# A fused attention and Strassen MLP kernel: q's cast moved to ScalarE, loads emitted as each group begins, weight sums spread over VectorE and GpSimd

## The chip, the cores and the metric

The kernel runs on one core of a Trainium2 chip. The metric is the device time of one execution in microseconds (us), the median over several runs. TensorE (PE) multiplies into PSUM, VectorE (DVE) and ScalarE (ACT) read PSUM and SBUF, GpSimd (POOL) works on SBUF, and SyncE (SP) issues most of the transfers.

## The reference

```python
def _attn_ref(q, k, v):                       # q, k, v: 8 x 8 x 576 x 64
    k_p = k.reshape(B, H, 72, 8, D).mean(axis=3)      # pooled by 8
    v_p = v.reshape(B, H, 72, 8, D).mean(axis=3)
    scores = np.matmul(q, k_p.transpose(0, 1, 3, 2)) / np.sqrt(D)
    ...                                       # softmax over the 72 pooled keys
    return np.matmul(attn, v_p)

def _moe_ref(x, w_in, w_out):                 # x: 4608 x 512, the heads side by side
    h = x @ w_in                              # 512 x 2048
    g = h - np.tanh(h)
    return g @ w_out                          # 2048 x 512
```

The attention of a batch gives 576 rows of x, and the MLP runs over all 4608 rows. Inputs and the output are float32.

## The kernel before

**Two things in step.** The MLP works on nine groups of 512 tokens (`g`), the attention on eight batches of 576 tokens. While group `g` is multiplied, batch `nb = g + 1` goes through scores and values, and batch `nn = g + 2` is loaded and pooled. x is kept transposed in a ring `xT` of three groups. The order of the instructions on each engine is the order in which the code emits them; a scheduler does not move them. Only waits between engines are put in by the framework.

**Stage one of a group: h.** `h_pair(g, p, ...)` multiplies xT with two 128-wide blocks of `w1b` into two PSUM banks (line 514), takes tanh on ScalarE (line 526) and subtracts on VectorE, which writes `Gt` (line 527). There are seven pairs, and `h_one` for the eighth. Four pairs of banks are in turn. VectorE then forms `P` (`sum_p`, line 535), `Q` (line 540) and `Dg` (line 545), the sums and differences of `Gt` that the output product needs.

**Stage two: the output product in Strassen's form (Winograd's variant).** Seven half-size products (`products`, line 582; matmuls in line 562) replace eight. They use the four quarters `b11, b12, b21, b22` of `w2b` and their sums. In the kernel before, three sums lie in `w2s` (b11+b22, b11+b12, b21+b22), and three quarters are overwritten in place: b21 by b21-b11, b12 by b22-b12, b22 by -b22. Five sums or differences are VectorE's (line 553), and the negation is ScalarE's (line 899). They run once, during group 0 and before group 1. `after_product` (line 592) takes the results from PSUM; GpSimd has one subtraction there (line 601).

**The attention of a batch between them.** k and v are pooled by additions on GpSimd (`pool_k`, lines 233 to 241, writes `kd`; `pool_v`, lines 251 to 275, writes `VB`); batches 0 and 1 take other paths. q is cast to bf16 on GpSimd (`q_cast`, lines 183 and 187) from `q_raw`, of which there are two buffers, into the one buffer `q_bf`. SyncE transposes by DMA: `kd` into `kT` (line 316), the five blocks of `q_bf` into `qT` (line 193). GpSimd places `kT` into `KB` (lines 284 to 288). `scores` (line 333) run after each of the first five half products of stage two, and the first needs `qT` and `KB`. `av` (lines 380 to 398) follows after half products 6, 7, 8, 9 and 11 and writes `x_sb`, of which there are four buffers; SyncE transposes each into `xT` (line 418).

**SyncE's queue in a group.** In order: the five xT transposes of batch `g` at the end of group `g - 1`, the stores of group `g - 1` (line 577, five to eight), `kT`, the five `qT` transposes, then the loads of batch `g + 2`: k in two transfers, v in five, q in two. This comes from the emission in the h stage, at `p == 4` (at `p == 1` in group 1, where the q transposes stand before the loop):

```python
if nb is not None and p == (1 if g == 1 else 4):
    k_dma_transpose(nb)
    if g > 1:
        q_dma_transpose(nb)
    k_place(nb, nc.gpsimd.tensor_copy)
    if nn is not None:
        next_loads(nn)           # load_k, load_v, load_q
```

Group 0 is written out by hand: its output product is the ordinary one (`mlp_o`, line 496), over sixteen steps `u`, and batch 1's attention, the first weight sums and the loads of batch 2 stand between the steps.

Of the kernel before, what the change touches and what calls it, by code (L numbers as in the profile page):

```python
# [42 lines left out]
def kernel(  # L43
# [14 lines left out]
    raw = ctx.enter_context(tc.tile_pool(name="raw", bufs=2))  # L58
# [38 lines left out]
    w2s = const.tile([128, 3, NP, HD], F16, name="w2s")  # L97
# [90 lines left out]

    def q_dma_transpose(b):
# [36 lines left out]

    def pool_k(b, eng, t0=0, t1=NT, mid=()):
        r = k_raw[b % 2].rearrange("p t (j d) -> p t j d", d=D)[:, t0:t1, :, :]
        if b not in kdups:
# [3 lines left out]
        first = eng.tensor_tensor(  # L233
            out=r[:, :, 0:4, :], in0=r[:, :, 0:4, :], in1=r[:, :, 4:8, :], op=ALU.add
        )
# [13 lines left out]
    def pool_v(b, eng):  # L249
        r = v_raw[b % 2].rearrange("p t (j d) -> p t j d", d=D)  # L250
        eng.tensor_tensor(  # L251
            out=r[:, :, 0:4, :], in0=r[:, :, 0:4, :], in1=r[:, :, 4:8, :], op=ALU.add
        )
# [7 lines left out]
        v_left(VB[b % 2], r[:, NM, 0:1, :], eng)  # L261
# [12 lines left out]
    def v_left(vb, vs, eng):  # L274
        eng.tensor_tensor(
# [129 lines left out]
    def new_x():  # L405
        return work.tile([128, 2, 4, D], BF16, name="x_sb", tag="x_sb", bufs=4)
# [145 lines left out]
    def w_sum(out, a, b, op):  # L552
        nc.vector.tensor_tensor(out=out, in0=a, in1=b, op=op)  # L553
# [5 lines left out]
    def product(bk, lhs, rhs, k0, k1, first):  # L559
        for k in range(k0, k1):  # L560
            for tt in range(2):
                nc.tensor.matmul(  # L562
                    PS[:, bk, tt * HD : (tt + 1) * HD],
                    lhsT=lhs(k, slice(tt * 128, (tt + 1) * 128)),
                    rhs=rhs[:, k, :],
                    start=(first and k == 0 and tt == 0),
# [4 lines left out]
    def chain(bk):  # L571
        return PS[:, bk, :].rearrange("p (t n) -> p t n", t=2)
# [6 lines left out]
    def sh(c, off):  # L579
# [3 lines left out]
        (C1, lambda k, c: Gt[:, k, 1, sh(c, HT)], b21),  # L583
        (C2, lambda k, c: P[:, k, sh(c, HT)], b11),
        (C1, lambda k, c: P[:, k, c], b22),
# [6 lines left out]
    def after_product(g, n):  # L592
        if n == 0:
            nc.scalar.copy(out=m4, in_=chain(C1))
        if n == 1:
            nc.vector.tensor_tensor(out=O[:, 2:4, 0:HD], in0=chain(C2), in1=m4, op=ALU.add)
            sum_d(0, 2)
            sum_d(2, 4)
        if n == 2:
            nc.scalar.copy(out=m45, in_=chain(C1))  # L600
# [3 lines left out]
        if n == 3:  # L604
            nc.vector.tensor_tensor(out=O[:, 0:2, HD:DM], in0=m4, in1=chain(C2), op=ALU.subtract)
        if n == 4:
            nc.scalar.copy(out=m451, in_=chain(C1))  # L607
            nc.vector.tensor_tensor(out=m451, in0=m451, in1=m45, op=ALU.subtract)
        if n == 5:
            nc.vector.tensor_tensor(  # L610
                out=O[:, 2:4, HD:DM], in0=m451, in1=chain(C2), op=ALU.subtract
# [100 lines left out]
    q_raws[1] = raw.tile([128, H, R + 1, D], FP32, name="q_raw", tag="q_raw")  # L712
    after(load_k(1), w1_dmas[1])
    load_q(1, False)
    load_main(v_pairs, v_raw[1], 1, 0, NM)
# [65 lines left out]
    load_q_tail(1, q_raws[1], nc.scalar)  # L781
# [215 lines left out]
```

## Time and profile before

| | |
|---|---|
| median of 3 runs | 317.17 us (316.47 to 318.3) |
| the profiled execution, its own time | 316.82 us |
| its span in the profile | 315.1 us |
| mean granted TensorE clock | 0.982 |
| PE busy | 284.5 us (90%), 2048 matmuls |
| DVE busy | 232.9 us (74%), 397 instructions |
| ACT busy | 140.5 us (45%), 225 instructions |
| POOL busy | 130.9 us (42%), 118 instructions |
| transfers on SyncE's queue | 42.94 MB, 54.8% of 16 DMA engines |

Times in the profile are microseconds from the start of the span. A line of a timeline has the start, the time, the engine, the line of the code, the operation with its output and inputs, and in brackets the time for which the engine had been idle and what ended that. "PEld" is the weight load of TensorE, "SPq" the issue of a transfer by SyncE. Groups 1 to 6 start their first h product at 56.30, 92.87, 124.72, 158.02, 191.10 and 222.27 us.

### The profile page before, as it was taken

How to read it: one execution, taken by the hardware profiler on the slowest of the kernel's cores; microseconds unless marked ns; L12 is line 12 of the kernel's file. 1: busy time of each engine (PE TensorE's matmuls, PEld its weight loads, DVE VectorE, ACT ScalarE, POOL GpSimd, SP SyncE). 2: the span in 40 equal slices, each digit the busy share in tenths (PEclk: the TensorE clock that was granted, in tenths of full speed). 3: DMA queues.
4: the chain of work that ended last, by engine and by line, in shares of the span. 5: the costliest groups of instructions: out<-in, count | busy, mean ns of one | idle time of the engine just before them, and what ended most of it. 6: DMA issues, size and time to landing. Idle time of an engine off the chain costs nothing.

```text
span 315.1 us, 5444 instructions
## 1 busy us (share of the span) xinstructions
PE 284.5 (90%) x2048; PEld 180.0 (57%) x2048; DVE 232.9 (74%) x397; ACT 140.5 (45%) x225; POOL 130.9 (42%) x118
## 2 busy tenths in 40 slices
PE   7999899839999799979899987999998999999980
PEld 3545455315884487438744872469546954864770
DVE  6658568968996968596858882799688948937950
ACT  4656664075516551555146511562465146136320
POOL 8501707870299129901991199107950100100010
PEclk9999999989999999999999997999999999999997
DMA  7999999569137499549965998589361260030004
GB/s 268 209 226 272 304 246 306 158 162 324 30 67 151 92 322 194 164 75 307 194 160 96 310 184 147 116 282 209 76 169 23 52 155 7 0 117 19 0 21 115
DMA packets 66538, 49.84 MB, mean 158 GB/s; under 512 B 40016, under 2 KB 53456, under 8 KB 66512
## 3 DMA queue, kind: packets, MB, share of 16 engines
q1 hardware_dynamic: 59104, 42.94, 54.8%
q0 software_dynamic: 4752, 4.72, 9.0%
q10 hardware_dynamic: 2656, 1.84, 2.1%
q8 instruction: 16, 0.26, 0.4%
q14 instruction: 10, 0.08, 0.1%
HBM read 36.70 MB, written 9.44 MB: 146 GB/s over the span
## 4 chain that ended last, share of the span: by engine, by line
PE 35%; POOL 22%; DMA 14%; DVE 13%; SPq 6%; issue 4%; ACT 2%; POOLq 0%; DVEq 0%; ACTq 0%
PE PS L562 18%; PE PS L514 9%; SPq L193 6%; DVE Gt L527 6%; DMA xT<-x_sb 4%; DMA w1b<-in_moe_w_in_dram 4%; POOL v_raw L251 4%; POOL k_raw L233 4%; DMA k_raw<-in_k_dram 3%; PE PS L333 3%; DMA qT<-q_bf 3%; PE PS L496 3%; POOL q_bf L183 2%; DVE w2b L553 2%; DVE P L535 2%
## 5 line engine op out<-in xcount | busy, mean ns | idle before, releaser
L514 PE MATMUL PS<-xT,w1b 128*128 128x512 bf16 x512 | 115.2, 386 | 12.3 <-DVE Gt L527 5.4
L527 DVE TENSOR_TENSOR Gt<-PS,TS 128x1024 bf16<-128x1024 f32 x56 | 68.3, 1222 | 36.9 <-ACT TS L526 36.9
L514 PEld LDWEIGHTS <-w1b 128*128 128x128 f16 x512 | 50.5, 99 | 74.4 <-issue 14.2
L526 ACT ACTIVATE TS<-PS 128x1024 f32<-128x1024 f32 x56 | 57.2, 1024 | 48.2 <-PE PS L514 46.4
L601 POOL TENSOR_TENSOR m<-O,m 128x512 f32<-128x512 f32 x8 | 10.4, 1306 | 129.2 <-DVE Dg L545 77.1
L398 DVE TENSOR_TENSOR x_sb<-PS,rden 128x256 bf16<-128x256 f32 x72 | 30.6, 425 | 6.3 <-DMA xT<-x_sb 3.9
L562 PE MATMUL PS<-w2b,Gt 128*128 128x256 f16 x256 | 33.2, 273 | 0.8 <-DVE Gt L532 0.7
L562 PE MATMUL PS<-w2b,P 128*128 128x256 f16 x256 | 32.3, 273 | 0.0
L233 POOL TENSOR_TENSOR k_raw<-k_raw 128x1280 f32<-128x1280 f32 x7 | 20.3, 2897 | 27.7 <-DMA k_raw<-in_k_dram 16.8
L562 PEld LDWEIGHTS <-Gt 128*128 128x128 bf16 x256 | 24.4, 98 | 7.5 <-DVE Gt L532 2.0
L562 PE MATMUL PS<-w2s,Dg 128*128 128x256 f16 x240 | 28.5, 273 | 0.0
L352 ACT ACTIVATE E<-PS 128x288 bf16<-128x288 f32 x60 | 21.8, 410 | 13.3 <-PE PS L333 13.2
L562 PEld LDWEIGHTS <-P 128*128 128x128 bf16 x256 | 24.5, 98 | 4.7 <-issue 1.4
L562 PEld LDWEIGHTS <-Dg 128*128 128x128 bf16 x240 | 23.0, 98 | 2.4
L333 PE MATMUL PS<-qT,KB 128*128 128x288 bf16 (+5 forms) x128 | 17.7, 289 | 5.8 <-DMA qT<-q_bf 5.7
L535 DVE TENSOR_TENSOR P<-Gt 128x1024 bf16<-128x1024 bf16 x32 | 22.0, 688 | 0.3
L545 DVE TENSOR_TENSOR Dg<-Gt 128x1024 bf16<-128x1024 bf16 x32 | 22.0, 751 | 0.0
L380 PE MATMUL PS<-VB,E 128*128 128x130 bf16 x240 | 20.2, 220 | 0.1
L380 PEld LDWEIGHTS <-E 128*128 128x128 bf16 x240 | 16.8, 98 | 1.9 <-issue 0.4
L607 ACT COPY m<-PS 128x512 f32<-128x512 f32 x8 | 4.7, 586 | 29.5 <-PE PS L562 29.5
L251 POOL TENSOR_TENSOR v_raw<-v_raw 128x1280 f32<-128x1280 f32 x6 | 17.3, 2883 | 0.0
L562 PE MATMUL PS<-w2s,Q 128*128 128x256 f16 x128 | 16.3, 273 | 0.0
(107 smaller groups left out, 345.5 us busy)
## 6 DMA issues: line engine op xcount, KB each, us to landing
k_raw<-in_k_dram SPq DMA_DIRECT2D x7, 1024.0 KB, 5.7
q_raw<-in_q_dram SPq DMA_DIRECT2D x7, 1024.0 KB, 10.2
v_raw<-in_v_dram SPq DMA_DIRECT2D x7, 1024.0 KB, 8.9
out_dram<-O SPq DMA_DIRECT2D x36, 128.0 KB, 2.4
out_dram<-O SPq DMA_DIRECT2D x16, 256.0 KB, 2.8
w1b<-in_moe_w_in_dram POOLq DMA_DIRECT2D x4, 512.0 KB, 13.7
w2b<-in_moe_w_out_dram POOLq DMA_DIRECT2D x4, 512.0 KB, 17.3
k_raw<-in_k_dram SPq DMA_DIRECT2D x7, 128.0 KB, 5.5
```

What stands on the lines that cost most here:

```text
L233: first = eng.tensor_tensor(out=r[:, :, 0:4, :], in0=r[:, :, 0:4, :], in1=r[:, :, 4:8, :], op=ALU.add)
L251: eng.tensor_tensor(out=r[:, :, 0:4, :], in0=r[:, :, 0:4, :], in1=r[:, :, 4:8, :], op=ALU.add)
L333: nc.tensor.matmul(dst[p : p + w], lhsT=KB[b % 2][:, o : o + w], rhs=qTs[b][:, m, c0:c1], start=True, stop=True,)
L352: nc.scalar.activation(out=E[:, t, half * hs : (half + 1) * hs], in_=ps[:, :], func=ACT.Exp, scale=SCALE)
L380: nc.tensor.matmul(ps[:, 2 * n : 2 * n + 2, :].rearrange("p h d -> p (h d)") if n < 2 else ps.rearrange("p (a s) d -> p a s d", s=2)[:, :, ...
L398: nc.vector.tensor_tensor(out=x_sb[:, half, :, :], in0=ps[:, :, 0:D], in1=rden[:, :, :].to_broadcast([128, 4, D]), op=ALU.mult,)
L514: nc.tensor.matmul(dst, lhsT=w1b[:, fb, i * 128 : (i + 1) * 128], rhs=xT[:, fb, c0 : c0 + TG], start=(fb == 0), stop=(fb == NFB - 1),)
L526: nc.scalar.activation(out=t2, in_=PS[:, b0 : b0 + 2, :], func=ACT.Tanh)
L527: nc.vector.tensor_sub(out=Gt[:, p, :, :], in0=PS[:, b0 : b0 + 2, :], in1=t2)
L535: nc.vector.tensor_tensor(out=P[:, a:b, :], in0=Gt[:, a:b, 0, :], in1=Gt[:, a:b, 1, :], op=ALU.add)
L545: nc.vector.tensor_tensor(out=Dg[:, a:b, :, :], in0=Gt[:, a:b, :, 0:HT], in1=Gt[:, a:b, :, HT:TG], op=ALU.subtract,)
L562: nc.tensor.matmul(PS[:, bk, tt * HD : (tt + 1) * HD], lhsT=lhs(k, slice(tt * 128, (tt + 1) * 128)), rhs=rhs[:, k, :], start=(first and k ...
```

## The change

It has six parts. (1) q's cast for batches 2 to 7 becomes `q_cast_part`, three instructions on ScalarE, emitted ahead of the first three h pairs (one pair later in group 1). (2) `raw` has one buffer instead of two, and batch 1's q and v loads are emitted later. (3) In the h stage, `k_dma_transpose`, `k_place`, `load_k` and `load_v` are emitted at `p == 0`, and `q_dma_transpose` and `load_q` after the third cast part. (4) The weight sums no longer work in place but for b12: `w2s` has five members. b21-b11 is made by GpSimd in four pieces, -b22 by ScalarE in two, b11+b22 and b21+b22 by VectorE in four and two pieces within group 1. (5) For batches from 2 on, the first addition of `pool_k` and of `pool_v` is two instructions, and `pool_k`, `pool_v` are emitted after half product 6 instead of 7. (6) `x_sb` has five buffers, and the last product of the last group has its own banks for its two halves and one store per segment instead of column halves.

```diff
-    raw = ctx.enter_context(tc.tile_pool(name="raw", bufs=2))
+    raw = ctx.enter_context(tc.tile_pool(name="raw", bufs=1))
-    w2s = const.tile([128, 3, NP, HD], F16, name="w2s")
+    w2s = const.tile([128, 5, NP, HD], F16, name="w2s")
+    def q_cast_part(b, n):
+        t = q_raws[b]
+        if n < 2:
+            nc.scalar.copy(
+                out=q_bf[:, 0:R, 4 * n : 4 * n + 4, :].rearrange("p j h d -> p h j d"),
+                in_=t[:, 4 * n : 4 * n + 4, 0:R, :],
+            )
+        else:
+            nc.scalar.copy(out=q_bf[:QT, R, :, :], in_=q_raws.pop(b)[:QT, :, R, :])
...
+    def halves(n, b):
+        return ((0, n),) if b < 2 else ((0, n // 2), (n // 2, n))
...
-        return work.tile([128, 2, 4, D], BF16, name="x_sb", tag="x_sb", bufs=4)
+        return work.tile([128, 2, 4, D], BF16, name="x_sb", tag="x_sb", bufs=5)
...
-        (C1, lambda k, c: Gt[:, k, 1, sh(c, HT)], b21),
+        (C1, lambda k, c: Gt[:, k, 1, sh(c, HT)], w2s[:, 3, :, :]),
-        (C1, lambda k, c: P[:, k, c], b22),
+        (C1, lambda k, c: P[:, k, c], w2s[:, 4, :, :]),
...
+            w_sum(w2s[:, 1, :, :], b11, b12, ALU.add)
+            v1_done = pool_v(1, nc.vector)
+            after(
+                [
+                    w_sum(w2s[:, 3, :, :], b21, b11, ALU.subtract, nc.gpsimd, k, k + 2)
+                    for k in range(0, NP, 2)
+                ],
+                v1_done,
+            )
...
+        if u in (9, 11):
+            n = (u - 9) // 2
+            nc.scalar.mul(
+                out=w2s[:, 4, 4 * n : 4 * n + 4, :], in_=b22[:, 4 * n : 4 * n + 4, :], mul=-1.0
+            )
...
     pool_k(2, nc.gpsimd)
-    q_cast(2)
     pool_v(2, nc.gpsimd)
-    q_dma_transpose(2)
-    w_sum(b21, b21, b11, ALU.subtract)
     w_sum(b12, b22, b12, ALU.subtract)
-    nc.scalar.mul(out=b22, in_=b22, mul=-1.0)
...
         for p in range(NP - 1):
+            c = p if g > 1 else p - 1
+            if nb is not None and 0 <= c < 3:
+                q_cast_part(nb, c)
             h_pair(g, p, (0, 2, 4, 6, 0, 2, 4)[p], p % 2)
+            if g == 1 and p < 4:
+                w_sum(w2s[:, 0, :, :], b11, b22, ALU.add, k0=2 * p, k1=2 * p + 2)
...
-            if nb is not None and p == (1 if g == 1 else 4):
+            if nb is not None and p == 0:
                 k_dma_transpose(nb)
-                if g > 1:
-                    q_dma_transpose(nb)
                 k_place(nb, nc.gpsimd.tensor_copy)
                 if nn is not None:
-                    next_loads(nn)
+                    load_k(nn)
+                    load_v(nn)
+            if nb is not None and c == 2:
+                q_dma_transpose(nb)
+                if nn is not None:
+                    load_q(nn)
...
+                if g == 1 and n in (1, 2):
+                    w_sum(w2s[:, 2, :, :], b21, b22, ALU.add, k0=4 * n - 4, k1=4 * n)
...
-                if u == 7 and nn is not None:
+                if u == 6 and nn is not None:
                     pool_k(nn, nc.gpsimd)
                     pool_v(nn, nc.gpsimd)
-                    q_cast(nn)
```

## The prediction

> **What bounds the kernel now.** I read the page's chain first, then TensorE's timeline for its idle gaps, then what the releaser of each gap was waiting for: the SyncE queue, VectorE and GpSimd. TensorE is busy for 284.5 of 315.1 us, so only its gaps can be won. These are the long ones from group 1 on, in its timeline (start, us, work; in brackets the idle time before it and its releaser):
>
> ```profile
> 56.30 7.08 PE L514 MATMUL PS<-xT,w1b 128*128 128x512 bf16 x32 [1.52 <-DVE O L505]
> 68.77 8.59 PE L514 MATMUL PS<-xT,w1b 128*128 128x512 bf16 x32 [5.39 <-DVE Gt L527]
> ...
> 109.82 0.28 PE L333 MATMUL PS<-qT,KB 128*128 128x288 bf16 x1 [1.98 <-DMA qT<-q_bf]
> ...
> 158.02 13.97 PE L514 MATMUL PS<-xT,w1b 128*128 128x512 bf16 x64 [1.68 <-DVE x_sb L398]
> ...
> 191.10 15.66 PE L514 MATMUL PS<-xT,w1b 128*128 128x512 bf16 x64 [3.36 <-DVE x_sb L398]
> ```
>
> Three kinds: group 1 waits for the weight sums (1.52 + 5.39); the scores wait for qT (1.98, and in the same view 2.07, 0.17, none and 1.47 in groups 3 to 6); the first h product waits for xT (0.33, 1.68, 3.36 at groups 3, 4, 5). The two gaps of over 3 us cost more than themselves. The windows view (us, then busy time of each engine, granted clock, DMA share, GB/s) shows half clock after both:
>
> ```profile
> 68.50:71.90 3.40, 3.13 (x8) 1.13 (x8) 3.38 (x4) 2.05 (x2) 1.05 (x4) 0.50 0.92 339
> 191.40:194.70 3.30, 3.30 (x10) 1.07 (x9) 0.26 (x1) 0.16 (x1) 3.14 (x5) 0.50 0.39 112
> ```
>
> Half clock for 3.4 us is 1.7 us of matmul lost; no gap of 2.07 us or less was followed by it. What feeds the scores is SyncE's queue; here it is for group 2, which starts at H = 92.87:
>
> ```profile
> 100.87 1.26 SPq L316 DMA_TRANSPOSE kT<-kd  x1
> 102.24 6.44 SPq L193 DMA_TRANSPOSE qT<-q_bf  x5
> 108.72 0.59 SPq L137 DMA_DIRECT2D k_raw<-in_k_dram  x1
> 109.78 0.65 SPq L146 DMA_DIRECT2D k_raw<-in_k_dram  x1
> 110.48 0.57 SPq L137 DMA_DIRECT2D v_raw<-in_v_dram  x1
> 111.10 1.93 SPq L141 DMA_DIRECT2D v_raw<-in_v_dram  x4
> ```
>
> The queue reaches the five q transposes only after the old group's xT transposes and its stores, and it goes straight from the transposes to the next loads. So qT lands at 109.8, when TensorE has already stood for 1.98 us.
>
> **Steady groups: the queue order.** The diff moves q's cast from GpSimd to ScalarE and emits the loads earlier in the group. In the built program SyncE's order becomes kT, two k loads, five v loads, five q transposes, two q loads: seven loads now stand ahead of the transposes. Two things follow. First their issue: from 108.72 to 113.03, 4.3 us (3.9 in the other groups). Second, a slot: the build gives SyncE's transfers eight semaphores in turn, and each waits for the transfer eight before it. The trace shows that wait, always at the ninth transfer after a k load, in the waits of SyncE's queue:
>
> ```profile
> SPq L162 <- DMA k_raw<-in_k_dram: 7.5, 6, 1.7
> ```
>
> With the new order the second transpose waits for k's main load, the third for k's rest, the fourth for v's main load, the fifth for v's first rest. Landing times are in the page's issues (KB each, median us to landing):
>
> ```profile
> k_raw<-in_k_dram SPq DMA_DIRECT2D x7, 1024.0 KB, 5.7
> ...
> v_raw<-in_v_dram SPq DMA_DIRECT2D x7, 1024.0 KB, 8.9
> ```
>
> Call E the end of kT's issue. v's main load is issued at E+1.4 (E+1.9 in group 2). Its landing took 7.6 to 10.4 us over the groups; I take 8.5, group 1's, where no xT transpose ran beside it. Then the fourth transpose starts at E+9.9, the fifth 1.3 later at E+11.2, and lands 2.5 us after its start: E+13.7 (bounds 12.8 and 16.1). Today it is E+7.7. E lies 9.3, 6.4, 7.4 and 6.8 us after H in groups 2 to 5 (102.13, 131.07, 165.44, 197.88 against H of 92.87, 124.72, 158.02, 191.10), because xT and the stores of the old group are unchanged. The second half of the first scores wants qT at H+15.0 (109.82 - 1.98 - 92.87). The stalls become 8.0, 5.1, 6.1 and 5.5 = 24.7 us, against 4.2 today: **+20.5**. Group 6 loads nothing more and keeps its 1.47.
>
> Each of these stalls is longer than 3.36, the shortest gap that was followed by half clock. Four dips at 1.7 are 6.8, less the one at 191.4 that goes: **+5.1**. If only two of the four fall, 3.4 less. The Trainium skill, page "TensorE: Matmul & The Clock Gate", section "What's actually happening", says that the gate looks at free-running windows of about 3.4 us and throttles after an idle one. By that rule a stall of 5 to 6 us need not cover a whole window; with two dips of four the sum by the rule would be 3.4 us smaller.
>
> The loads now end before the xT transposes are issued (the last, q's, at about E+13 and landing some 6 us later; the first xT is issued 8.2 us after the scores resume, 118.04 against 109.82). Their waits at the heads of groups 3 to 5 go: 0.33 + 1.68 + 3.36 = **-5.4**. The fifth x_sb buffer serves the same wait and is priced in it.
>
> The Trainium skill, "DMA: Bandwidth & Descriptors", section "Queues, rings and completion order", speaks against the new order too: each DMA engine consumes one issuing queue's descriptors in ring order. It also says that completion need not be in that order, so by the page alone a transpose could land beside v's loads; the sum would then be the second rival's below.
>
> **The casts.** Three per batch on ScalarE, by this row of its groups (busy, mean ns):
>
> ```profile
> L183 ACT CAST q_bf<-q_raw 128x1024 bf16<-128x1024 f32 x2 | 2.0, 1042 | 1.8 <-DMA q_raw<-in_q_dram 1.8
> ```
>
> 1.04 + 1.04 + 0.61 beside a tanh of 1.02 for each pair. ScalarE idles 0.70 per pair, so two pairs overrun by 0.34 each; VectorE idles 0.5 behind it and TensorE has four pairs of banks. I count nothing; uncovered it would be 0.7 in each of six groups. GpSimd loses 1.9 + 0.6 per batch, off the path in the new order. Its split first additions add an instruction each, some 0.1 us, covered the same way. One q buffer makes q's load wait for the casts, done by about H+5.5 and long before SyncE gets there; batch 1's load waits for a cast that ended at 21.1 instead of issuing at 20.27, behind k's load that lands at 29.95.
>
> **Group 1: the weight sums.** Today VectorE and GpSimd block each other here:
>
> ```profile
> 57.41 7.20 DVE L553 TENSOR_TENSOR w2b<-w2b 128x2048 f16<-128x2048 f16 x2
> ...
> 56.20 2.93 POOL L183 CAST q_bf<-q_raw 128x2048 bf16<-128x2048 f32 x1 [1.63 <-DMA q_raw<-in_q_dram]
> 59.08 1.60 POOL L187 CAST q_bf<-q_raw 64x512 bf16<-64x512 f32 x1
> 60.65 2.88 POOL L251 TENSOR_TENSOR v_raw<-v_raw 128x1280 f32<-128x1280 f32 x1
> 63.60 2.40 POOL L254 TENSOR_TENSOR v_raw<-v_raw 128x640 f32<-128x640 f32 x1
> ```
>
> Two sums of 1.21 alone took 7.20: each waited out a whole GpSimd instruction, and GpSimd in turn (1.60 for 0.55). Then ScalarE's negation (1.91) stood ahead of the first tanh. Afterwards one 1.21 sum stands before the group, at the price of one GpSimd instruction (up to 1.5). The b11+b22 sum is four pieces between the pairs (about 0.35, estimated as a quarter of 1.21 and 0.05 of start, each up to 1.7 of waiting), the negation lies in ScalarE's idle 3.0 us before 49.46, and b21-b11 goes to GpSimd: four pieces at some 1.2 (its 128x512 rows are 1.05 and 1.31) in the idle 10.9 us before 48.44. They push the pooling of batch 2 back by 2 to 3 us. Laid out in order VectorE is the bound: it ends the last Gt half near 73.3 instead of 78.5, with product 0's first half already issued; that moves the product stage 5.8 us forward. The b21+b22 sum (two of 0.65) and its waits behind GpSimd then delay x_sb of batch 2 by about 1 at the end. I take **-4.8**; bounds -2.5 (every piece waits its longest) and -6.9 (both gaps go whole).
>
> **Tail.** SyncE's last row has two stores instead of three (1.82 us for three): **-0.5**. The last product's own banks remove gaps of 0.46 and 0.35 that end before SyncE's stores do: nothing.
>
> **Sum:** +20.5 + 5.1 - 5.4 - 4.8 - 0.5 = +14.9. The profiled execution took 316.82 (its span 315.1 and 1.7 around it; median 317.17), so 331.7; I say 330, for the dips may not all fall.
>
> **Rivals.** *On time (faster).* The transposes land no later than now, since loads and stores drain before SyncE needs them. For it: 2.3 MB is some 7 us at the 330 GB/s of the load windows. Against: the slot wait, and xT transposes issued behind q's loads today took 5.7 to 9.2 us to land instead of 2.3. Price: -4.8 - 5.4 - 1.7 - 0.5 = -12.4, 304; 300 if the qT stalls go too. *Only the issue counts (slower, less).* Transposes begin 3.9 us late and land at E+11.6: stalls 5.9, 3.0, 4.0, 3.4 = 16.3, three dips; +12.1 + 3.4 - 5.4 - 4.8 - 0.5 = +4.8, 322. The change breaks even when the fifth transpose lands about 2 us later than now, near E+10, without dips. *The lock stays (slower, more).* Pieces meet GpSimd every time and v lands at 10.4: +2.3 + 9.6 on the sum, 343.
>
> **Numbers.** Main case 0.63 (323 to 338), issue only 0.14, on time 0.15, break-even 0.06, lock 0.02. Within 0.5% (about what a measurement here can tell from no change) 0.06; faster 0.15; slower 0.79. The range 314 to 340 leaves out the on-time case and the outer ends.
>
> **What would show it.** Right: TensorE's gap before the first scores of groups 2 to 5 at 5 to 8 us, released by qT; SyncE's fourth q transpose waiting for v_raw; half clock after them; group 2's h products beginning near 88; no xT gaps. Wrong: qT gaps of 2 us or less, or q transposes landing by E+9.

## The result, and the profile after

| | before | after |
|---|---|---|
| median | 316.82 us (315.29 to 318.3, 4 runs) | **335.76 us** (333.61 to 336.62, 4 runs) |
| profiled execution | 316.82 us, span 315.1 | 335.3 us, span 333.6 |
| mean granted TensorE clock | 0.982 | 0.946 |

The ratio is 1.0588, with a 95% interval of 1.0515 to 1.0661: the changed kernel is slower. The four runs of before are those taken beside the changed kernel. Medians and ranges here and below are over all executions of a kernel; the ratios leave out those that were over 1.5% longer than the fastest of the same kernel.

TensorE's timeline after the change, read as before (start, us, work; in brackets the idle time before it and its releaser):

```profile
56.52 13.99 PE L529 MATMUL PS<-xT,w1b 128*128 128x512 bf16 x64 [0.67 <-DVE O L520]
...
87.89 13.99 PE L529 MATMUL PS<-xT,w1b 128*128 128x512 bf16 x64 [0.85 <-DMA xT<-x_sb]
...
109.56 0.40 PE L348 MATMUL PS<-qT,KB 128*128 128x288 bf16 x1 [6.81 <-DMA qT<-q_bf]
110.99 0.42 PE L348 MATMUL PS<-qT,KB 128*128 128x288 bf16 x1 [1.03 <-DMA qT<-q_bf]
147.81 0.40 PE L348 MATMUL PS<-qT,KB 128*128 128x288 bf16 x1 [4.91 <-DMA qT<-q_bf]
149.26 0.40 PE L348 MATMUL PS<-qT,KB 128*128 128x288 bf16 x1 [1.05 <-DMA qT<-q_bf]
186.86 0.40 PE L348 MATMUL PS<-qT,KB 128*128 128x288 bf16 x1 [6.06 <-DMA qT<-q_bf]
188.54 0.42 PE L348 MATMUL PS<-qT,KB 128*128 128x288 bf16 x1 [1.28 <-DMA qT<-q_bf]
223.82 0.40 PE L348 MATMUL PS<-qT,KB 128*128 128x288 bf16 x1 [4.58 <-DMA qT<-q_bf]
225.27 0.42 PE L348 MATMUL PS<-qT,KB 128*128 128x288 bf16 x1 [1.05 <-DMA qT<-q_bf]
```

Group 1's h stage is one unbroken run of 64 matmuls now, and group 2 starts at 87.89 instead of 92.87. The xT gaps at the heads of groups 3 to 5 are gone. In their place the first scores of groups 2 to 5 wait for qT twice each: once for the blocks of the first half of the tokens, once for the rest. Here is SyncE's queue that feeds them, group 2 (H, the start of its first h product, is 87.89):

```profile
96.26 1.27 SPq L331 DMA_TRANSPOSE kT<-kd  x1
97.58 0.57 SPq L137 DMA_DIRECT2D k_raw<-in_k_dram  x1
98.20 0.63 SPq L146 DMA_DIRECT2D k_raw<-in_k_dram  x1
98.88 0.58 SPq L137 DMA_DIRECT2D v_raw<-in_v_dram  x1
99.50 2.26 SPq L141 DMA_DIRECT2D v_raw<-in_v_dram  x4
101.87 7.97 SPq L203 DMA_TRANSPOSE qT<-q_bf  x5
109.89 0.58 SPq L170 DMA_DIRECT2D q_raw<-in_q_dram  x1
```

Seven loads went ahead of the five transposes, which begin at 101.87. The chain of waits around that place (start, us, what) goes through v's main load and the fourth transpose, issued as v lands, to the fifth:

```profile
98.88 8.47 DMA v_raw<-in_v_dram
...
107.36 1.19 SPq L203
...
108.65 2.29 DMA qT<-q_bf
...
110.99 0.42 PE PS L348
```

And the waits of SyncE's queue (line, releaser, us in total, times, longest) name k's and v's loads for the transposes of L203; this wait did not exist before:

```profile
SPq L203 <- DMA v_raw<-in_v_dram: 6.4, 5, 1.6
...
SPq L203 <- DMA k_raw<-in_k_dram: 3.2, 5, 1.2
```

Last, the windows view (us, then busy time of each engine with its instructions, granted clock, DMA share, GB/s) around the stalls of groups 2 and 4:

```profile
102.70:106.10 3.40, 0.05 (x1) 0.00 (x0) 3.37 (x6) 0.00 (x0) 0.00 (x0) 1.00 0.97 325
106.20:109.50 3.30, 0.00 (x0) 0.00 (x0) 0.01 (x1) 0.00 (x0) 0.00 (x0) 0.50 1.17 183
109.60:112.90 3.30, 2.27 (x10) 1.38 (x11) 0.00 (x0) 0.82 (x2) 0.00 (x0) 0.50 0.55 154
113.00:116.30 3.30, 3.30 (x17) 2.27 (x16) 0.00 (x0) 1.91 (x5) 0.00 (x0) 0.50 0.69 211
116.50:119.80 3.30, 3.30 (x36) 2.55 (x35) 2.67 (x5) 1.70 (x5) 0.00 (x0) 1.00 0.00 0
...
184.70:188.00 3.30, 0.40 (x1) 0.10 (x1) 0.00 (x0) 0.41 (x1) 0.00 (x0) 0.50 0.71 138
188.10:191.40 3.30, 2.86 (x14) 1.99 (x15) 0.00 (x0) 1.05 (x3) 0.00 (x0) 0.50 0.78 249
191.60:195.00 3.40, 3.40 (x36) 2.63 (x35) 1.53 (x3) 2.00 (x7) 0.00 (x0) 1.00 0.37 88
```

The clock falls to half 3 to 4 us into the stall and stays there after the stall is over: at group 2 for three stretches of 3.4 us, at the other groups for two. The fourth row shows the price: 17 matmuls in 3.30 us of unbroken work, against 36 in the row after it.

Read in finer windows, the clock falls at 106.18, 147.14, 184.69 and 222.23 and comes back at 116.42, 153.97, 191.51 and 229.06. Any two of these moments lie a whole number of stretches of 3.41 us apart (from 116.42 to 147.14 it is nine): the clock changes only on a fixed grid. Laid over TensorE's busy time, such a grid fits the profiles of both kernels and of all experiments but the first kernel of experiment 4. From group 1 on, every stretch at full clock in which TensorE was busy for 1.47 of 3.41 us or less was followed by half clock (47 stretches, the ends of the kernels included), and none of the 912 with 1.48 or more was. So two short gaps in one stretch can do what one long gap does.

Where the time went, by the starts of the groups (H of groups 1, 2, 3, 4, 5 and 6: 56.30, 92.87, 124.72, 158.02, 191.10, 222.27 before; 56.52, 87.89, 128.05, 165.95, 204.39, 241.52 after):

| group | 1 | 2 | 3 | 4 | 5 | 6 to the end |
|---|---|---|---|---|---|---|
| before, us | 36.57 | 31.85 | 33.30 | 33.08 | 31.17 | 92.83 |
| after, us | 31.37 | 40.16 | 37.90 | 38.44 | 37.13 | 92.08 |
| difference | -5.2 | +8.3 | +4.6 | +5.4 | +6.0 | -0.8 |

With +0.2 ahead of group 1 this is the 18.5 us between the spans. Group 1 and the tail gain, the four groups that load ahead of qT lose 24.2.

### The profile page after: what moved, and what is told of

Read it like the earlier page. It is cut to its first block, busy times and chain, and to the rows that moved or that the text cites. A ratio compares the mean times of both kernels' runs of the same rounds, so it can differ in the third digit from the quotient of the medians.

```text
span 333.6 us, 5456 instructions
## 1 busy us (share of the span) xinstructions
PE 291.2 (87%) x2040; PEld 183.4 (55%) x2040; DVE 228.9 (69%) x400; ACT 154.3 (46%) x244; POOL 122.4 (37%) x122
## 4 chain that ended last, share of the span: by engine, by line
PE 43%; DMA 16%; DVE 14%; POOL 11%; SPq 6%; issue 4%; ACT 3%; ACTq 1%; POOLq 0%
PE PS L585 19%; DMA v_raw<-in_v_dram 11%; PE PS L529 10%; DVE Gt L542 5%; PE PS L511 4%; DMA qT<-q_bf 3%; PE PS L348 3%; POOL v_raw L266 3%; POOL k_raw L247 3%; DVE Dg L560 2%; PE PS L395 2%; PE PS L483 2%; DMA q_raw<-in_q_dram 2%; SPq L602 2%; DVE P L550 2%
## 5 line engine op out<-in xcount | busy, mean ns | idle before, releaser
L529 PE MATMUL PS<-xT,w1b 128*128 128x512 bf16 x512 | 111.8, 379 | 1.5 <-DMA xT<-x_sb 0.9
L626 POOL TENSOR_TENSOR m<-O,m 128x512 f32<-128x512 f32 x8 | 11.1, 1388 | 154.9 <-DVE Dg L560 89.8
L348 PE MATMUL PS<-qT,KB 128*128 128x288 bf16 (+5 forms) x128 | 20.9, 316 | 28.3 <-DMA qT<-q_bf 28.0
L621 DVE TENSOR_TENSOR O<-PS,m 128x512 f32<-128x512 f32 x8 | 5.5, 690 | 38.4 <-ACT E L367 38.1
L585 PEld LDWEIGHTS <-Gt 128*128 128x128 bf16 x256 | 26.1, 104 | 9.1 <-DVE Gt L547 2.1
L585 PEld LDWEIGHTS <-P 128*128 128x128 bf16 x256 | 26.4, 105 | 6.7 <-issue 1.4
L247 POOL TENSOR_TENSOR k_raw<-k_raw 128x512 f32<-128x512 f32 (+2 forms) x13 | 21.6, 1681 | 16.1 <-DMA k_raw<-in_k_dram 16.1
L348 PEld LDWEIGHTS <-KB 128*128 128x128 bf16 (+1 forms) x128 | 7.8, 102 | 34.4 <-issue 25.6
L585 PE MATMUL PS<-w2s,Gt 128*128 128x256 f16 x128 | 20.3, 310 | 1.3 <-DVE Gt L547 1.3
L585 PE MATMUL PS<-w2b,P 128*128 128x256 f16 x128 | 19.5, 306 | 0.0
L266 POOL TENSOR_TENSOR v_raw<-v_raw 128x512 f32<-128x512 f32 (+1 forms) x12 | 19.2, 1620 | 0.0
## 6 DMA issues: line engine op xcount, KB each, us to landing
w1b<-in_moe_w_in_dram POOLq DMA_DIRECT2D x4, 512.0 KB, 13.7
```

The costliest lines, as they stand in the source:

```text
L247: first = eng.tensor_tensor(out=r[:, ta:tb, 0:4, :], in0=r[:, ta:tb, 0:4, :], in1=r[:, ta:tb, 4:8, :], op=ALU.add)
L266: eng.tensor_tensor(out=r[:, ta:tb, 0:4, :], in0=r[:, ta:tb, 0:4, :], in1=r[:, ta:tb, 4:8, :], op=ALU.add)
L348: nc.tensor.matmul(dst[p : p + w], lhsT=KB[b % 2][:, o : o + w], rhs=qTs[b][:, m, c0:c1], start=True, stop=True,)
L529: nc.tensor.matmul(dst, lhsT=w1b[:, fb, i * 128 : (i + 1) * 128], rhs=xT[:, fb, c0 : c0 + TG], start=(fb == 0), stop=(fb == NFB - 1),)
L585: nc.tensor.matmul(part(g, bk, tt), lhsT=lhs(k, slice(tt * 128, (tt + 1) * 128)), rhs=rhs[:, k, :], start=(first and k == 0 and (tt == 0 o ...
```

## The experiments

The theory: the whole loss is the loads that stand ahead of qT, first as a stall, then as half clock; everything else in the change is a gain or nothing. The rivals: the casts, the single q buffer or the spread weight sums cost something of their own; or only SyncE's issue time and slot waits matter, not the bytes.

**1. The loads alone taken back behind qT.**

```diff
             if nb is not None and p == 0:
                 k_dma_transpose(nb)
                 k_place(nb, nc.gpsimd.tensor_copy)
-                if nn is not None:
-                    load_k(nn)
-                    load_v(nn)
             if nb is not None and c == 2:
                 q_dma_transpose(nb)
                 if nn is not None:
+                    load_k(nn)
+                    load_v(nn)
                     load_q(nn)
```

> Changed kernel with one edit: the k and v loads are emitted behind the q transposes instead of ahead of them; casts on ScalarE, one q buffer and the new weight sums stay. Theory (the queue order is the whole loss): the qT stalls of groups 2 to 5 fall from 26.8 us in all to 5 or less, the half clock after them goes (9 us), the xT waits of before (up to 5.4 us) may come back; 302 to 309 us. Rival (the casts on ScalarE or the single q buffer hold the transposes): the stalls stay, within 3 us of 335.

Measured: 307.43 us (305.27 to 309.29), 0.9677 of before (0.9613 to 0.9742). The longest gap in front of scores is now group 2's:

```profile
103.99 0.28 PE L348 MATMUL PS<-qT,KB 128*128 128x288 bf16 x1 [2.61 <-DMA qT<-q_bf]
```

Moving seven loads behind five transposes in one queue takes 28 us off the changed kernel, and what is left of the change beats the kernel before. The median landing of a qT transpose goes from 3.4 us (up to 7.8) to 2.5 (up to 4.3).

**2. The loads alone put ahead of qT in the kernel before.**

```diff
                 k_dma_transpose(nb)
+                k_place(nb, nc.gpsimd.tensor_copy)
+                if nn is not None:
+                    load_k(nn)
+                    load_v(nn)
                 if g > 1:
                     q_dma_transpose(nb)
-                k_place(nb, nc.gpsimd.tensor_copy)
                 if nn is not None:
-                    next_loads(nn)
+                    load_q(nn)
```

> Kernel before with one edit: in groups 2 to 5 the k and v loads are emitted between the k transpose and the q transposes; q's cast stays on GpSimd, two q buffers, old weight sums. Theory: the same stalls as in the changed kernel (about +22 us), the same dips of the clock (+7 to +9), the xT waits go (-5): 338 to 344 us. Rival (the order is harmless by itself): 315 to 320 us.

Measured: 341.56 us (340.16 to 342.71), ratio 1.074 (1.0671 to 1.0808). The gaps in front of the scores are 7.83 + 1.19, 4.92 + 1.03, 5.57 + 0.89 and 5.05 + 1.32 us, as in the changed kernel; group 1 keeps two gaps (1.03 and 5.39), no xT gap is left. So this one edit of the order brings the loss by itself, and takes the xT waits away by itself.

**3. Small loads first, so that no transpose waits for a slot.** v's four small loads and k's rest are issued first, k's and v's main loads last ahead of qT; then each transpose's eighth predecessor has landed when its turn comes.

```diff
-                    load_k(nn)
-                    load_v(nn)
+                    load_left(v_pairs, v_raw[nn % 2], nn)
+                    load_dense(k_pairs, k_raw[nn % 2], nn)
+                    load_main(k_pairs, k_raw[nn % 2], nn, 0, NM)
+                    load_main(v_pairs, v_raw[nn % 2], nn, 0, NM)
```

> Changed kernel with the loads ahead of the q transposes reordered: the four small v transfers and k's rest first, k's and v's main loads last, the same bytes. The second to fifth q transposes then wait for the small transfers' slots. Theory that the bytes ahead in the queue count most: the first gap before the scores stays at 4.5 to 7 us, and the second one, about 1.05 us each, goes: 329 to 333 us. Rival (the slot wait is the price): transposes issue at once and land some 3 us earlier in each group: 318 to 324 us.

Measured: 338.31 us (337.17 to 339.46, 2 runs), ratio 1.0652 (1.0568 to 1.0737): a miss. TensorE's timeline at group 2, and below it SyncE's queue:

```profile
113.63 0.40 PE L348 MATMUL PS<-qT,KB 128*128 128x288 bf16 x1 [10.42 <-DMA qT<-q_bf]
114.28 0.42 PE L348 MATMUL PS<-qT,KB 128*128 128x288 bf16 x1 [0.25 <-DMA qT<-q_bf]
```

```profile
102.20 0.49 SPq L137 DMA_DIRECT2D v_raw<-in_v_dram  x1
102.81 10.29 SPq L203 DMA_TRANSPOSE qT<-q_bf  x5
```

The slot wait is worth the second gap only: that fell from 1.03 to 0.25 us (0.32, 0.27 and 0.22 in the later groups). The first gap grew to 10.42, 6.15, 6.86 and 6.56, since the main loads start 3 to 4 us later than in the changed kernel (v's at 102.20 instead of 98.88). v's load took 9.8 us and landed at 112.0; the first transpose, issued at its heels, landed at 112.5. The issue of the transposes was slow as well: 2.04 us each in the median and up to 3.01, where the median in the kernel before is 1.26, so that the fifth left at 111.9 without having waited for a slot. From v's issue to the second scores it is 12.1 us in both kernels (98.88 to 110.99, 102.20 to 114.28). It is when the bytes are through that decides, with or without a slot wait.

**4. TensorE kept busy through the stalls.** Unused matmuls of 512 columns ahead of the first scores of groups 2 to 5: 20 each in the first kernel, 30, 22, 26 and 20 in the second. The stalls themselves stay.

```diff
+                if u == 0 and nn is not None and g > 1:
+                    for _ in range({2: 30, 3: 22, 4: 26, 5: 20}[g]):     # first kernel: range(20)
+                        nc.tensor.matmul(
+                            PS[:, 4, :], lhsT=ident[:, :], rhs=w1b[:, 0, 0:512], start=True, stop=True
+                        )
```

> Changed kernel with 20 matmuls of 512 columns, which nobody reads, ahead of the first scores of groups 2 to 5: 4.3 us of work inside each stall. Theory (the half clock after the stalls is a price of its own, about 2.3 us per group): the stall's end does not move, the clock stays at 1.00, 325 to 328 us. Rival (the slow stretch after the stall has another cause, such as transfers beside the matmuls): within 2 us of 335.

> The changed kernel with unused matmuls of 512 columns ahead of the first scores of groups 2 to 5, as e4_filler, but 30, 22, 26 and 20 of them, so that they cover the stalls of 6.8 + 1.0, 4.9 + 1.1, 6.1 + 1.3 and 4.6 + 1.1 us more closely. The stalls themselves stay, only TensorE is kept busy in them. The theory (each stall costs a second time, in half clock after it): the four stretches at half clock go, 9 us come back, but some matmuls overshoot the stall by 0 to 1 us each; 327.5 us (325.5 to 330), mean clock 0.975 or more. The rival (half clock is not caused by TensorE's idling): the clock stays near 0.946 and the time at 335 or more.

Measured: 331.47 us with 20 each (331.01 to 331.92 in three executions, 392.15 in the fourth, the profiled one, at a clock of 0.753; ratio 1.0432, 1.0374 to 1.049), slower than the 325 to 328 expected; 329.19 us with the fitted numbers (328.1 to 330.29, 2 runs; ratio 1.046, 1.0352 to 1.0568), as expected. In the profile of the second kernel the clock holds at groups 2 to 4; at group 5, behind the gaps of 1.49 and 1.43 that were left, it falls for one stretch (220.30 to 223.71). The window of group 2 that stood at 0.50:

```profile
113.00:116.30 3.30, 3.30 (x37) 2.56 (x35) 2.42 (x5) 1.98 (x7) 0.00 (x0) 1.00 0.60 164
```

The mean clock is 0.986. Of 335.76 us, 6.6 come back (by the spans, 333.6 and 328.6, 5.0). The fillers overshoot the stalls a little: 98 of them at 0.221 us are 21.7, and with the gaps that remain (0.35 + 1.13, 0.72 + 1.15, 0.80 + 1.04, 1.49 + 1.43) TensorE spends 29.8 us there, against 26.8 in the changed kernel. So the half clock that went was worth 8.0 to 9.6 us, and the stretch that was left costs up to 1.7 more. TensorE's idling is its cause, since the stalls and the transfers stayed and only TensorE's work in them was altered.

**5. The parts alone, on the kernel before.** The weight sums, with the one q buffer that they need for room (and so batch 1's q and v loads where the change has them); and the casts of batches 3 to 7 on ScalarE.

```diff
+            if g == 1 and p < 4:                                   # sums alone
+                w_sum(w2s[:, 0, :, :], b11, b22, ALU.add, k0=2 * p, k1=2 * p + 2)
...
+            if g > 1 and nb is not None and p < 3:                 # casts alone
+                q_cast_part(nb, p)
...
-                    q_cast(nn)
```

> The kernel before, with the weight sums alone as in the change (five members of w2s, pieces on GpSimd, ScalarE and VectorE) and what they need of room: one q_raw buffer, so batch 1's q and v loads and batch 2's q load stand where the change has them. The casts, the order of SyncE's queue in a group, four x_sb buffers and the pooling stay as before. The theory (the sums are worth about -5, in group 1 alone, and the loss of the change is all from the loads ahead of qT): group 2's first h product starts near 88 us instead of 92.87, the gaps of 1.52 and 5.39 us and the half clock behind them are gone, the other groups keep their gaps of qT (about 2 us at groups 2 and 3) and of xT (1.7 and 3.4 us at groups 4 and 5); 312 us (310 to 315). The rival (the sums are what costs: pieces that lock with GpSimd, one q buffer that holds q's load back): no gain in group 1, qT gaps of over 4 us, 317 or more.

> The kernel before, with q's cast for batches 3 to 7 alone moved to ScalarE ahead of the first three h pairs (batch 2's stays on GpSimd); two q_raw buffers, and SyncE's order as before (kT, the five qT, then all loads). The theory (the casts on ScalarE cost nothing and take only GpSimd's part of the wait): group 3's qT gap of 2.07 us, where GpSimd's cast ended after kT, shrinks by up to 2, no new gap appears behind the tanhs; 315.5 us (313 to 317.5). The rival (casts ahead of the tanhs hold the h pairs up by 0.7 to 2.7 us in each of five groups): gaps in the h stage and 321 to 330.

Measured: the sums 311.11 us (308.75 to 315.61, 10 runs), ratio 0.9839 (0.9787 to 0.9891), about -5; the casts 314.73 us (313.36 to 319.47, 10 runs), ratio 0.9981 (0.9919 to 1.0042), no difference. With the sums, group 2 starts at 88.17, by a profile that is the longest of their ten runs. Groups 2, 3, 5 and 6 keep their gaps (2.59, 1.94, 3.56 and 1.49), and group 4 has 1.48 in front of its scores in place of 1.68 at its head. With the casts, group 3's qT gap of 2.07 is gone and group 2's is 0.61 + 2.12; no gap appears in the h stages of the groups that have the casts. So neither the casts nor the sums with their single q buffer cost time. The rest of the change (the pooling, `x_sb`, the tail) was not run alone; experiment 1, which has all of it, is faster than before.

**6. Half a dose: k's loads alone ahead of qT.**

```diff
                 k_place(nb, nc.gpsimd.tensor_copy)
                 if nn is not None:
                     load_k(nn)
-                    load_v(nn)
...
                 q_dma_transpose(nb)
                 if nn is not None:
+                    load_v(nn)
                     load_q(nn)
```

> The changed kernel with k's two loads (1.2 MB) alone ahead of the five qT transposes, v's five loads behind them. A half dose. The theory (the time by which qT lands late goes by the issue and the bytes of the loads ahead): the fifth qT lands some 10 us after kT's issue instead of 13.4, so the stalls of groups 2 to 5 fall by about 3 us each, to 4.8, 2.8, 4.1 and 2.4, with half clock behind two of them; 318 us (312 to 323). A rival (only the slot of v's main load, for which the fourth transpose waits, makes qT late): no wait of a transpose for a load is left, so the stalls become those of e1_loads_behind plus the issue of two loads, under 2.5 us in all but group 2, and 310 us or less. The other rival (any load ahead costs the whole stall): 330 or more.

Measured: 315.16 us (313.78 to 317.83), ratio 0.9981 (0.9916 to 1.0046). The gaps are 3.94 + 0.52, 2.75, 1.60 + 0.75 and 0.75 + 0.82, of which the 1.60 ends with a Gt of VectorE. No transpose waits for a load's slot, and the time lies between experiment 1 (307) and the changed kernel (336): 1.2 MB ahead cost about 8 us, the other 1.1 MB about 20 more. The gaps of groups 2 to 5 sum to 11.1 us against 26.8, and the mean clock is 0.975 against 0.946. Half clock follows three of the stalls, for one stretch each, where two were expected. Both rivals miss: the first said 310 or less, the second 330 or more.

**7. Experiment 1 with the old group's stores, too, behind qT.**

```diff
                 q_dma_transpose(nb)
+            if g > 1 and p == 2:
+                store(g - 1, 1)
+                store(g - 1, 0)
+            if nb is not None and c == 2:
                 if nn is not None:
                     load_k(nn)                 # load_v(nn), load_q(nn)
...
-            if u == 12:
-                store(g, 1)
...
-            store(g, 0)
```

> The changed kernel with k's and v's loads behind the five qT transposes, as in e1_loads_behind, and besides with the old group's stores taken from ahead of kT to between qT and the loads. Nothing is left out. The theory (what stands ahead of qT on SyncE's queue sets its landing, stores too): kT and qT start 3 to 6 us earlier, the qT gaps that e1_loads_behind still has (2.61, 0.20 and 1.21 us) go, the loads and the xT transposes behind them stay where they were, so the xT gaps of 0.8, 0.7 and 2.4 us may stay; 303.5 us (301 to 306). The rival (the stores are not in the way, since kT waits for GpSimd's pooling, or O's buffer comes free too late and VectorE's write of O waits for the stores): 307 or more, with gaps in the product stage.

Measured: 313.58 us (311.88 to 315.02), ratio 0.9918 (0.9865 to 0.9971): slower than experiment 1, a miss in time. All qT gaps went, as expected, but TensorE's timeline has this instead:

```profile
121.90 15.66 PE L529 MATMUL PS<-xT,w1b 128*128 128x512 bf16 x64 [4.54 <-DMA xT<-x_sb]
...
155.76 15.66 PE L529 MATMUL PS<-xT,w1b 128*128 128x512 bf16 x64 [2.52 <-DMA xT<-x_sb]
...
190.54 15.66 PE L529 MATMUL PS<-xT,w1b 128*128 128x512 bf16 x64 [3.46 <-DMA xT<-x_sb]
```

The stall moved to the other set of transposes. The scores are not late any more, so xT is issued earlier (111.64 instead of 113.88 in group 2), while q's load, ahead of it, is issued later (108.07 instead of 106.81) and takes 11.9 us to land instead of 9.3. The xT transposes of that group then landed up to 9.2 us after their issue, against 4.5 in experiment 1.

**8. The main loads on ScalarE's queue.** k's and v's main loads are issued by ScalarE at the place where the change has them, the small loads and q's by SyncE behind qT; the second kernel has the stores behind qT as well.

```diff
                 if nn is not None:
-                    load_k(nn)
-                    load_v(nn)
+                    load_main(k_pairs, k_raw[nn % 2], nn, 0, NM, nc.scalar)
+                    load_main(v_pairs, v_raw[nn % 2], nn, 0, NM, nc.scalar)
...
                 q_dma_transpose(nb)
+                                               # second kernel: store(g - 1, 1), store(g - 1, 0) here
                 if nn is not None:
+                    load_dense(k_pairs, k_raw[nn % 2], nn)
+                    load_left(v_pairs, v_raw[nn % 2], nn)
                     load_q(nn)
```

> The changed kernel with the two large loads of a batch (k main and v main, 1 MB each) issued by ScalarE at the same place in the group, on its own queue; k's rest, v's rest and q's loads are issued by SyncE behind the qT transposes. The same bytes move at about the same time or some us earlier, but nothing stands ahead of qT on SyncE's queue. If it is the order on one queue that makes qT late: qT lands 2.3 to 4 us after its issue although 2 MB are under way, the stalls at groups 2 to 5 are those of e1_loads_behind (2.6 us at group 2, under 1 us after), the xT gaps shrink since the loads end earlier; ScalarE's issues may wait for a store, up to 3 us ahead of a tanh; 306 us (302 to 312). If it is the bytes on the 16 engines, by whatever queue they come: qT lands 5 to 7 us after its issue while the loads run, with stalls of 3 to 5 us at each of the four groups; 322 us (316 to 328).

> e10_act_queue with the old group's stores taken behind the qT transposes, as in e7_stores_last; nothing is left out. If the order on one queue decides: qT's gaps go as in e7_stores_last, and the xT gaps that were 4.5, 2.5 and 3.5 us there (the xT transposes stood behind 3.5 MB of loads on the queue) fall to under 1 us each, since only q's 1.2 MB is still ahead of them; 303 us (299 to 307). If the bytes decide: gaps of qT of 2 to 4 us, xT gaps smaller than in e7_stores_last because the loads end earlier; 315 us (309 to 322).

The first: 325.44 us (325.16 to 326.61), ratio 1.0347 (1.0289 to 1.0406), within the second side's range, but for another reason. ScalarE's timeline in group 2:

```profile
89.73 0.37 ACTq L137 DMA_DIRECT2D k_raw<-in_k_dram  x1
98.26 0.37 ACTq L137 DMA_DIRECT2D v_raw<-in_v_dram  x1
98.68 1.04 ACT L192 CAST q_bf<-q_raw 128x1024 bf16<-128x1024 f32 x1 [8.00 <-DMA out_dram<-O]
```

v's load went out only when a store of the old group had landed (issued at 90.17, 8.0 us to landing), and with it ScalarE, its casts and its tanhs had to wait: TensorE stood 5.48, 2.58, 4.07 and 4.08 us in the h stages of groups 2 to 5, waiting for Gt. The first scores had no gap, but only because they came late. This kernel does not tell the two sides apart.

The second kernel has no store between, and is the fastest of all: **300.14 us** (299.62 to 303.68), ratio 0.9574 (0.9473 to 0.9675), clock 0.990, TensorE busy for 94% of the span, no gap of over 0.9 us from group 1 on. Its time is that of the first side, but its landings are those of the second. From the DMA views of group 2, taken where ScalarE issues v and where SyncE issues the first qT (KB, us to landing):

```profile
v_raw<-in_v_dram ACTq DMA_DIRECT2D x1, 1024.0 KB, 10.2
kT<-kd SPq DMA_TRANSPOSE x1, 10.1
...
qT<-q_bf SPq DMA_TRANSPOSE x1, 8.8
```

v was issued at 90.30 and the first qT at 92.14, on another queue with no load ahead. They land at 100.5 and 100.9. So it isn't only the order of one queue that holds the transposes back: bytes under way on another queue do so too. How the two share the DMA engines is in the view of 96 to 98 us (queue, packets, MB, share of 16 engines; q10 is ScalarE's queue, q1 SyncE's):

```profile
q10 hardware_dynamic: 333, 0.68, 87.1%
q1 hardware_dynamic: 334, 0.09, 18.8%
```

They moved packet for packet, but a packet of the load was 2.0 KB and one of the transposes some 0.3 KB, so the transposes got an eighth of the bytes. The Trainium skill, page "DMA: Bandwidth & Descriptors", section "Queues, rings and completion order", says that each DMA engine goes round its queues packet by packet, and these two rows agree with that. It does not explain the whole 8.8 us: from 94 to 95.4 us SyncE's queue moved 9 packets and ScalarE's 269.

The gain is one of time. kT leaves at 90.36 instead of 96.26 and the loads at 89.8 instead of 97.6, so k's and v's main loads are through ten us before the next xT transposes (111.31), and qT is there when the scores want it at 102.51.

**9. The stores alone behind qT, all loads on SyncE's queue ahead of it.** This asks what the second queue brings beside the earlier start.

```diff
                 q_dma_transpose(nb)
+            if g > 1 and p == 2:
+                store(g - 1, 1)
+                store(g - 1, 0)
...
-            if u == 12:
-                store(g, 1)
...
-            store(g, 0)
```

> The changed kernel with the old group's stores alone taken behind the qT transposes: SyncE's order becomes kT, the seven loads of k and v, the five qT, the stores, q's loads. All loads stay on SyncE's queue, but start where e11_act_queue_stores has them on ScalarE's. If the start of the bytes is all (a second queue brings nothing): kT leaves 2.4 to 5.4 us earlier than in the changed kernel, the fifth qT lands 13.4 us after it, the stalls fall to about 2.4, 1.9, 3.3 and 3.2 us with half clock behind two at most, no xT gap over 1 us, 311 us (306 to 316). If ScalarE's queue brings something of its own in e11_act_queue_stores, the distance to its 300.1 is that: the slots that the transposes wait for, and seven issues less ahead of them. If it brings nothing at all, not even by the slots: 300 to 304. If the stores behind qT collide with VectorE's write of O, a gap in the product stage and 316 or more.

Measured: 317.46 us (315.54 to 320.72, 10 runs), ratio 1.0051 (1.0006 to 1.0095), 1.5 over the expected range. The gaps in front of the scores of groups 2 to 5 are 1.62 + 1.89, 2.12 + 0.68, 1.48 + 1.30 and 1.38 + 1.18, in sum 11.7 us where 10.8 were expected; the first of them ends with a Gt of VectorE, and half clock follows at groups 3, 4 and 5, for one stretch each. SyncE's queue in group 2:

```profile
90.80 1.93 SPq L331 DMA_TRANSPOSE kT<-kd  x1
92.78 0.58 SPq L137 DMA_DIRECT2D k_raw<-in_k_dram  x1
...
96.74 9.03 SPq L203 DMA_TRANSPOSE qT<-q_bf  x5
```

So the stores in front of kT were 18 of the 36 us between the changed kernel and the fastest. The rest is the second queue together with the five small loads, which stand behind qT there; the two were not run apart. The second queue doesn't free the transposes of the loads' bytes; it lets both leave sooner. The transposes leave at 92.14 instead of 96.74 and k's load at 89.83 instead of 92.78, because ScalarE issues the loads while SyncE is still busy with xT. That is 3 to 4.6 us, where the stalls here are 2.6 to 3.5.

## Why the prediction was right, point by point

The forecast was 330 us in a range of 314 to 340, slower with 0.79; measured were 335.76. Its sum by steps was +14.9 on the profiled execution, and the profile shows +18.5:

| step | predicted | shown by the profile after |
|---|---|---|
| stalls for qT, groups 2 to 5 (4.2 before) | 8.0, 5.1, 6.1, 5.5: +20.5 | 7.84, 5.96, 7.34, 5.63: +22.6 |
| half clock after them, less the one at 191.4 | +5.1 | +7.5 |
| xT waits at groups 3 to 5 | -5.4 | -5.4 |
| group 1 | -4.8 | -5.0 at group 2's start |
| tail | -0.5 | -0.8 from group 6 on |

The right column adds up to +18.9, 0.4 more than the spans show.

**The queue order: right.** v's main load landed 9.8 us after the end of kT's issue (E = 97.53), predicted 9.9; the fifth transpose landed at E+13.4, predicted 13.7; the wait for v's slot is in the chain at the fourth transpose. But the picture behind these numbers was half of the truth: the slot was taken for the cause, and experiment 3 shows that without it the transposes land no earlier, since they wait for v's bytes all the same. It came to the same number because the slot opens when the bytes are through. Of the rivals, *only the issue counts* would have had stalls of 16.3 us in all, and 26.8 were there; *on time* falls with the first of them.

**Half clock: the mechanism right, the size wrong.** This is the mis-sized term. I priced four dips at one stretch of 3.4 us, 1.7 each, from the two dips before, which followed gaps of 5.39 and 3.36. In the profile after, the half clock goes on until TensorE has worked through one stretch of 3.4 us nearly whole. At group 4 a stretch with 2.86 of 3.30 us busy is enough, at group 2 one with 2.27 is not, and the gap of 1.03 us in it (the second wait for qT) brings a third stretch. Before, the clock fell about when the work came back (at 68.48 and 191.36, with work from 68.77 and 191.10), so the first stretch was nearly all work and was the only one. Here it fell 0.7 to 3.4 us ahead of the first scores, and the second gap lay behind them, so the first stretch never counted. Work done at half clock after the first scores is 5.8, 5.1, 3.4 and 4.2 us (the stretches end 6.83, 6.13, 4.63 and 5.2 us after the scores' first matmul, less the second gaps); half of it is lost: 9.2 us instead of 6.8, and less 1.7 for the dip that went +7.5. Experiment 4, which takes the dips of groups 2 to 4 away and shortens the last, gives 8.0 to 9.6. The Trainium skill, page "TensorE: Matmul & The Clock Gate", section "What's actually happening", asks for a busy window of about 3.4 us before the throttle is released. I used its rule for the fall alone, which might have halved the dips; its rule for the release is what lengthened them, and the rows above agree with it. The doubt that made 331.7 into 330, that the dips may not all fall, went the wrong way.

**The casts: right.** Twelve of 1042 ns and six of 609 on ScalarE, no gap behind the tanhs, and no difference in time by themselves (experiment 5).

**Group 1: right,** and for the reason given. The rows of VectorE's timeline and one of GpSimd's:

```profile
56.38 2.25 DVE L568 TENSOR_TENSOR w2b<-w2b 128x2048 f16<-128x2048 f16 x1
...
60.71 1.50 DVE L568 TENSOR_TENSOR w2s<-w2b 128x512 f16<-128x512 f16 x1
...
63.27 1.07 DVE L568 TENSOR_TENSOR w2s<-w2b 128x512 f16<-128x512 f16 x1
...
66.94 0.41 DVE L568 TENSOR_TENSOR w2s<-w2b 128x512 f16<-128x512 f16 x1
```

```profile
45.59 4.50 POOL L568 TENSOR_TENSOR w2s<-w2b 128x512 f16<-128x512 f16 x4 [8.52 <-DVE VB L290]
```

The b12 sum took 1.0 more than its 1.21 alone, the first two pieces 1.1 and 0.7 more than the last; the four pieces on GpSimd lay in its idle time. The delay of x_sb of batch 2 that I put at 1 shows as the 0.85 in front of group 2; experiment 5, the sums alone, has 0.87 there. Experiment 5 gives the whole group as -5.

**xT's waits: right,** and experiment 2 shows that the loads' order alone removes them. What I did not see is that this is the same room changing hands: experiment 7 wins the qT gaps and gets the xT gaps back.

## What to carry to other kernels

Here a transpose by DMA landed as late as the large loads that were under way when it was issued, whichever queue they were on: draw each group's transfers on one line, with the moments at which the transposes are wanted, and put the large loads into the longest stretch between them; here the place of seven loads in one queue was worth 28 us, and a second queue for the two large ones, with the stores out of the way, 7 more. Price a stall of TensorE with its tail: half clock until one stretch of about 3.4 us has been worked through nearly whole, so that a second, small gap soon after the stall can cost a stretch more. Under 3 us, length alone does not tell whether the clock falls: a gap of 1.94 us did it in experiment 5's sums and one of 2.81 did not in its casts; what told was how little TensorE worked in a stretch of the grid. And where a load is issued from an engine with other work, look at what that issue can wait for: one store stopped ScalarE for 8 us.

## What the runs showed of the hardware that was not expected

- A transposing transfer on SyncE's queue took 8.8 us to land beside 2 MB on ScalarE's queue, against 2.3 to 2.5 alone; kT took 10.1 us in the same place.
- The clock did not come back with the end of a stall: 6.8 us at half clock at groups 3 to 5, 10.2 at group 2, where a stretch that was busy for 2.27 of 3.30 us did not count. In all profiles, stretches that brought it back were busy for 2.6 of 3.4 us or more, and one of 2.7 did not.
- The clock falls and comes back on a grid of 3.41 us, and falls after a stretch in which TensorE was busy for 1.47 us or less.
- Issuing the small loads first (experiment 3) put off v's main load by 3.3 us, from 98.88 to 102.20, and its landing by 4.6, from 107.4 to 112.0.

Left open: why the transposes' queue hardly moved a packet at first in experiment 8, before the two queues went packet for packet, and why their issue slows in experiment 3. The runs show that the transposes land with the loads, on one queue or on two, and only in part why.
